# A decode kernel's TensorE loop split into two nested halves, with zero products ahead of its first tile

## The chip, the cores and the metric

The kernel runs on one core of one Trainium2 chip. The metric is device time in microseconds (us) of one execution. The spans in the profiles are about 2 us shorter than these times; they run from the first to the last instruction.

## The reference, cut to what matters

Four sequences decode one token each. Attention has 16 query heads that share 8 key/value heads, with 8192 cached positions of width 256. A small MLP branch gates the result.

```python
q = (xn @ wq)                                  # 4 x 16 heads x 256
scores = einsum("bhqd,bhkd->bhqk", q, k) * 256 ** -0.5
o = einsum("bhqk,bhkd->bhqd", softmax(scores), v)
s = o @ wo
g = silu(mlp(xn))                              # w3, w4 (448 x 1792, 1792 x 448)
return x + s * g
```

There are 4 x 8 = 32 pairs of sequence and key/value head; "head h" below means one of these, 0 to 31. Each needs 4 MB of K and 4 MB of V, and these make up nearly all of the 279 MB that the kernel reads.

## The kernel before: the parts that matter

One queue (SyncE) issues all large loads in program order. There are two buffers for K and two for V. A K load for head h may be issued only when head h-2 has been transposed and evacuated, that is, copied out of TensorE's output memory by VectorE or ScalarE (`v_k` counts this).

```python
def load_k(h):
    if h >= 2:
        sp.wait_ge(S["v_k"], h - 1)
    sp.dma_start(kn_dst(h), A_k_cache[b, g]...)         # 4 MB
...
load_k(0); load_k(1)
load_wo(NLATE, HQ, "dwo")                               # 2.6 MB
for h in range(2, NH):
    load_k(h)
    load_v(h - 2)
# ... cut: the last two V loads, and the last 0.9 MB of wo
```

TensorE transposes K in 16 groups of 8 tiles (`f_t`, which takes the K semaphore at group 0), multiplies the transposed tiles with q (`f_s`), and runs the V products of head h-2 (`f_pv`) at the end of the body. Its loop holds two heads, and the last section, `finish()`, lies inside the loop. The 17th turn runs it and every other turn jumps over it.

```python
def body(h):
    for j in range(NGR):                                # 16 groups
        f_t(h, j)
        if j >= LAG: f_s(h, j - LAG)
        # ... cut: small f32 products of head h-1
    # ... cut: the last f_s, interleaved with f_pv(h - 2, ...)

with nc.Fori(0, NH // 2 + 1, engines=[e], head_slot={e: 64}) as it:
    with pe.If(it != NH // 2):
        body(0)
        body(1)
    with pe.If(it == NH // 2):
        finish()
```

`head_slot` is a parameter for where the loop's first instruction is placed.

## Time and profile before

| quantity | before | where read |
|---|---|---|
| time, median of the first 3 runs | 661.8 us | timed runs |
| span of the profiled run | 658.8 us | page |
| bytes read | 279 MB, 424 GB/s | page |
| TensorE busy | 84% | page, part 1 |
| distance from head to head, heads 6 to 31 (median) | 19.43 us | timeline |
| distance between landings of 4 MB loads in that stretch | 9.71 us (432 GB/s) | landing records |

**Which engine limits.** The DMA queue does. TensorE's busy share is high, but before nearly every head TensorE waits for that head's K. This is the list of waits of the kernel before (engine, line, what it waited for: total us, times, longest):

```profile
PE pst L582 <- PEq L243: 84.9, 29, 6.5
```

The reader is to see 29 waits, nearly one per head. Line 243 is the helper that records every semaphore wait, so the line does not say which wait it was. The trace's landing records do (each 4 MB load has 16 landing records there, and its landing is the last of the 16): from head 6 on each of these waits ends 0.14 us after the landing of that head's K. With a wait of 1.8 to 4.6 us per head, TensorE work saved in the middle of the run only lengthens the wait.

**Where the queue ran dry.** The timeline of TensorE in the kernel before shows two odd places (columns: start us, us, engine, line, operation, output<-inputs, shape, count, [idle before <- releaser]):

```profile
23.67 0.60 PE L572 MATMUL psm<-ou_f,selb 128*32 128x112 f32 x8 [0.82 <-PEq L243]
30.80 1.87 PE L582 MATMUL pst<-ident_b,kn 128*128 128x128 bf16 x16 [6.53 <-PEq L243]
...
48.18 1.05 PE L582 MATMUL pst<-ident_b,kn 128*128 128x128 bf16 x16
...
66.01 0.27 PE L602 MATMUL psm<-ident_f,rmax 128*2 128x128 f32 x1
72.75 1.87 PE L582 MATMUL pst<-ident_b,kn 128*128 128x128 bf16 x16 [6.47 <-PEq L243]
```

Head 0 starts slowly, 1.87 us for 16 transposes against 1.05 us for head 1, after 6.53 us of idle time. The clock granted to TensorE is either 0.5 or 1.0 of the full one in the trace's clock records. Here the first record is 1.0 from 37.15 us on; there is none before it. Head 2, the first after the loop's back edge, waits 6.47 us although its K had landed at 58.6 us; then it too takes 1.87 us for 16 transposes, and here the records show 0.5, from 71.28 to 78.11 us. Both delay the issue of a K load. These are the issues in SyncE's timeline, kernel before:

```profile
44.99 0.33 SPq L201 DMA_DIRECT2D kn<-in_A_k_cache_dram  x1
...
86.53 0.33 SPq L201 DMA_DIRECT2D kn<-in_A_k_cache_dram  x1
```

They are K of head 2 and K of head 4. By the landing records the loads ahead of them in the queue were complete at 47.22 us (wo) and 87.78 us (V of head 1), so each was issued only 2.23 and 1.25 us ahead. What that did can be seen in stretches of the kernel before (columns: stretch in us and its length, busy us of PE, PEld, DVE, ACT and POOL with their instructions, granted clock, DMA share, GB/s):

```profile
38.00:48.00 10.00, 10.00 (x210) 8.31 (x207) 4.57 (x9) 4.37 (x5) 0.00 (x0) 1.00 0.99 349
85.00:90.00 5.00, 5.00 (x104) 3.23 (x100) 1.97 (x4) 1.02 (x1) 0.00 (x0) 1.00 0.69 242
140.00:155.00 15.00, 12.51 (x268) 10.56 (x263) 6.98 (x15) 6.62 (x10) 0.32 (x2) 1.00 1.02 439
```

The last column is the point: 242 GB/s around 87 us against 439 later. Counted by landings, wo to K of head 2 took 11.35 us and V of head 1 to K of head 4 took 10.90 us, where 9.71 is normal. That is 1.64 + 1.19 = 2.8 us.

### The profile page before, as it was taken

The numbers are of one execution on the slowest core, as the hardware profiler recorded it, in microseconds if no ns is written. First come the engines' busy times: TensorE is split into PE (matmuls) and PEld (weight loads), VectorE is DVE, ScalarE is ACT, GpSimd is POOL, SyncE is SP. The second block draws the span as 40 slices with busy tenths as digits, with TensorE's granted clock in tenths as the row PEclk, the third lists the DMA queues.
The fourth block names the chain that finished last, engine by engine and source line by source line (L and its number), as shares of the span: only waits on it lengthen the run. The fifth ranks groups of instructions, "written<-read, shape, count | busy, mean of one in ns | idle before, by whom it ended". The sixth has DMA issues, their size and how long they took to land. (4 is left out here: it accounts for less than half of the span.)

```text
span 658.8 us, 22917 instructions
## 1 busy us (share of the span) xinstructions
PE 550.9 (84%) x9941; PEld 474.2 (72%) x9941; DVE 274.3 (42%) x593; ACT 256.1 (39%) x364; POOL 13.6 (2%) x77
## 2 busy tenths in 40 slices
PE   2499699987888988888988888998888898878896
PEld 1388588875767876676887766887676688757774
DVE  7344255543444343334443444444344344433441
ACT  4044255542334443334443433444333444423440
POOL 2000000000000000000000000000000000000000
PEclk9998799997898788799877899888789987978998
DMA  8999989999999999999999999999999999999997
GB/s 363 441 382 424 432 366 444 418 444 430 430 444 416 446 414 446 424 436 440 420 442 418 444 418 442 436 426 440 420 444 416 444 428 434 434 426 442 418 429 296
DMA packets 12369, 279.13 MB, mean 424 GB/s; under 512 B 1220, under 2 KB 3272, under 8 KB 3784
## 3 DMA queue, kind: packets, MB, share of 16 engines
q1 hardware_dynamic: 12336, 278.99, 99.0%
q8 instruction: 7, 0.11, 0.1%
q14 instruction: 2, 0.02, 0.0%
q10 hardware_dynamic: 24, 0.01, 0.0%
HBM read 278.99 MB, written 0.00 MB: 424 GB/s over the span
## 5 line engine op out<-in xcount | busy, mean ns | idle before, releaser
L582 PE MATMUL pst<-ident_b,kn 128*128 128x128 bf16 x4096 | 349.3, 240 | 84.9 <-PEq L243 84.9
L293 ACT ACTIVATE kT<-pst 128x1024 bf16<-128x1024 bf16 x224 | 229.3, 1024 | 364.5 <-ACTq L243 363.6
L582 PEld LDWEIGHTS pst<-ident_b,kn 128*128 128x128 bf16 x4096 | 277.3, 108 | 90.4 <-issue 89.8
L291 DVE COPY kT<-pst 128x1024 bf16<-128x1024 bf16 x288 | 197.5, 692 | 268.2 <-DVEq L243 268.2
L594 PE MATMUL psc<-qc,kT 128*128 128x2 bf16 x4096 | 179.0, 164 | 0.9 <-issue 0.8
L594 PEld LDWEIGHTS psc<-qc,kT 128*128 128x128 bf16 x4096 | 158.2, 98 | 29.7 <-issue 29.2
L638 PE MATMUL psv<-vb,pT 128*4 128x512 bf16 x1056 | 86.0, 378 | 1.3 <-PEq L243 1.2
L612 PE MATMUL psm<-sel,po 128*128 128x2 f32 x272 | 36.6, 257 | 0.0
L612 PEld LDWEIGHTS psm<-sel,po 128*128 128x128 f32 x272 | 34.7, 196 | 0.0
L638 PEld LDWEIGHTS psv<-vb,pT 128*4 128x4 bf16 x1056 | 21.8, 82 | 16.7 <-issue 2.0
L451 DVE TENSOR_REDUCE rmax<-psc 128x2 f32<-128x128 f32 x32 | 9.3, 292 | 48.1 <-DVEq L243 48.1
L469 DVE COPY po<-psv 128x512 f32<-128x512 f32 x34 | 23.5, 692 | 4.9 <-DVEq L243 4.1
L456 DVE TENSOR_REDUCE gmax<-psm 2x1 f32<-2x128 f32 x32 | 8.9, 279 | 35.2 <-DVEq L243 35.2
L315 ACT ACTIVATE pT<-psc,negb 128x64 bf16<-128x64 f32 x66 | 20.6, 331 | 5.4 <-ACTq L243 5.4
L606 PEld LDWEIGHTS psm<-diag,ones_f 2*128 2x128 f32 x66 | 14.0, 262 | 6.5 <-issue 5.6
L278 POOL COPY qc<-qT 128x4 bf16<-128x4 bf16 x32 | 5.9, 186 | 589.1 <-DVEq L468 573.0
L606 PE MATMUL psm<-diag,ones_f 2*128 2x2 f32 x66 | 16.7, 320 | 1.1 <-PEq L243 0.9
L315 ACT ACTIVATION_READ_ACCUMULATOR pT<-psc,negb 128x1 f32 x66 | 13.6, 206 | 0.0
L602 PEld LDWEIGHTS psm<-ident_f,rmax 128*2 128x2 f32 x32 | 2.6, 80 | 14.0 <-issue 14.0
L624 PE MATMUL psm<-rowsum,ones_f 128*128 128x2 f32 x66 | 12.0, 251 | 0.0
L533 PE MATMUL pst<-ident_b,xn_b 4*128 4x4 bf16 x14 | 0.6, 161 | 11.6 <-DVE xn_b L364 6.9
L624 PEld LDWEIGHTS psm<-rowsum,ones_f 128*128 128x128 f32 x66 | 9.8, 188 | 0.4 <-issue 0.4
(95 smaller groups left out, 96.5 us busy)
## 6 DMA issues: line engine op xcount, KB each, us to landing
kn<-in_A_k_cache_dram SPq DMA_DIRECT2D x32, 4096.0 KB, 25.6
vb<-in_A_v_cache_dram SPq DMA_DIRECT2D x31, 4096.0 KB, 30.8
vb<-in_A_wq_dram SPq DMA_DIRECT2D x1, 3584.0 KB, 11.3
vb<-in_B_w_dram SPq DMA_DIRECT2D x2, 1568.0 KB, 16.4
wo_sb<-in_A_wo_dram SPq DMA_DIRECT2D x1, 2688.0 KB, 43.8
kn<-in_A_v_cache_dram SPq DMA_DIRECT2D x1, 2048.0 KB, 25.0
kn<-in_A_v_cache_dram SPq DMA_DIRECT2D x1, 1024.0 KB, 27.0
kn<-in_A_v_cache_dram SPq DMA_DIRECT2D x2, 512.0 KB, 28.2
```

The costliest lines, as they stand in the source:

```text
L291: engine.tensor_copy(dst, src).then_inc(S["v_ev"], 1)
L293: engine.activation(dst, src, ACT.Copy).then_inc(S["a_ev"], 1)
L315: ins = act.activation(pv_p[:, :, hh], sc[:, :, hh], ACT.Exp, bias=negb[:, s, hh:hh + 1], scale=SCALE, accum_out=rowsum[:, s, hh:hh + 1])
L451: v.tensor_reduce(rmax[:, :], psc[h % 2][:, 0:NCH * REP].rearrange("p (k h) -> p h k", h=REP), AX.X, ALU.max).then_inc(S["v_rmax"], 1)
L456: v.tensor_reduce(gmax[:, :], psm[0:REP, 0:P], AX.X, ALU.max).then_inc(S["v_s"], 1)
L469: v.tensor_copy(po[:, slot], psv[:, 0:CP * DH]).then_inc(S["v_po"], 1)
L582: ins = pe.transpose(dst[:, t * P:(t + 1) * P], kn[:, h % 2, GC * j + kl, half * P:(half + 1) * P], ident_b[:, :])
L594: ins = pe.matmul(psc[h % 2][:, kk * REP:(kk + 1) * REP], kT[:, j % RING, t * P:(t + 1) * P], qc[:, h % 2, half, :], start=(half == 0), st ...
L606: pe.matmul(psm[:, P:P + REP], ones_f[0:REP, :], diag[:, :], start=True, stop=True).then_inc(S["p_m2"], 1)
L612: ins = pe.matmul(dst(dh)[:, 0:width], po[:, slot, i * DH + dh:(i + 1) * DH:NHALF], sel[:, i, 0:width], start=(i == 0), stop=(i == CP - 1))
L624: pe.matmul(psm[:, P + REP:P + 2 * REP], ones_f[:, :], rowsum[:, h % 2, :], start=True, stop=True)
L638: ins = pe.matmul(psv[o:o + CP * REP, 0:CP * DH], pT[:, h % 2, kk * REP:(kk + CP) * REP], src[:, kk:kk + CP, :].rearrange("p c d -> p (c d)"),
```

## The change

The inner loop now holds only the two bodies, so its back edge goes straight from the end of the body to its head. The jump over `finish()` comes once, after 16 heads. Eighteen matrix products with zero weights, whose result is overwritten later, fill the time in which TensorE waited for the first K. `head_slot` moves from 64 to 104 with them.

```diff
+    NWARM = 18
...
+            for i in range(NWARM):
+                pe.matmul(psv[0:PVW, 0:QW], pT[:, 0, 0:PVW], wq_sb[:, 0, 0:QW], start=True, stop=True)
...
-            with nc.Fori(0, NH // 2 + 1, engines=[e], head_slot={e: 64}) as it:
-                with pe.If(it != NH // 2):
+            with nc.Fori(0, 2, engines=[e]) as part:
+                with nc.Fori(0, NH // 4, engines=[e], head_slot={e: 104}):
                     body(0)
                     body(1)
-                with pe.If(it == NH // 2):
+                with pe.If(part == 1):
                     finish()
```

## The prediction

> **What bounds the kernel.** The DMA queue. The page gives 279 MB and 424 GB/s over a 658.8 us span. The timeline shows heads 6 to 31 starting every 19.42 us, and before each of them TensorE idles 1.8 to 4.6 us until that head's K has landed. The landings in the trace come every 9.71 us per 4 MB load, 432 GB/s. A TensorE head that does not wait takes 14.9 us (89.7 to 104.6). So nothing saved inside a steady head can show; only moments when the queue has run dry can be recovered.
>
> **Where the queue ran dry.** From the landing of the big wo load (47.2 us) to that of head 6's K (137.5 us) nine 4 MB loads landed in 90.3 us, where 9 x 9.71 = 87.4 would do: 2.9 us lost, in two places.
> 1. K of head 2 landed 11.35 us after wo, 1.65 too many. It was issued at 44.99 us, only 2.2 us before wo had landed, because head 0 ran slowly: 16 transposes take 1.87 us there against 1.05 later. The clock records show full speed only from 37.1 us. TensorE had been idle from 24.3 to 30.8 us.[...]
> 2. K of head 4 landed 10.9 us after V of head 1, 1.2 too many. It was issued at 86.5 us, just as the queue emptied, because TensorE stood from 66.3 to 72.75 us (6.47 us, timeline) at the first end of the loop body, although that head's K had landed at 58.6. The instruction queue moved a 16 KB block at 69.6 us: the jump over finish() went to a block not yet fetched, and head 2 then started at half clock. No block is fetched after 76.2 us, so later jumps are cheap (0.23 us at 105.0).
>
> **The change.** The inner loop's back edge goes from the body's end to an already loaded head, so the 6.5 us stall disappears in iteration 0; head 2 starts near 65 us at full clock and issues K of head 4 about 11.7 us later (as head 3 does), near 77 us, about 9 us before the queue is empty. The jump over finish() comes at head 16; even if it costs 6.5 us again, TensorE idles about 3 us there anyway and K is issued some 17 us before the queue needs it: no cost. The 18 zero products fill 24.3 to 30.7 us (0.43 us each at half clock, estimated from the 512-column products, so 4 to 7.7 us). At worst they delay the first tile 1.3 us; head 0 then runs at full clock and issues K of head 2 near 42.7 us, 4 to 5 us ahead of the queue's end.
>
> **Time.** On the critical path: 1.65 + 1.2 = 2.85 us. Everything later moves forward by that; the end (last V pieces and wo, DMA paced) is unchanged. 661.8 - 2.8 = 659.0 us; 8 in 10: 657.4 to 661.0. Chances: faster by over 2% 0.01, within 2% 0.98, slower 0.01.
>
> **What would show it.** First 16 transposes about 1.1 us; no gap near 66 us; head 2 about 8 us earlier; K of head 2 landing near 57, of head 4 near 96; still 19.42 us per head; waits for K per head unchanged or longer. Perhaps one long wait near head 16.
>
> **What would make it wrong.** The zero products not lifting the clock; instruction blocks arriving every 7.1 us holding the now faster first pass[...]; the shifted loop no longer staying resident, with fetches each iteration.

Two passages are cut, where marked, because no trace or run shows them: a rule about the clock, and a figure for how long the work of one instruction block takes. (The lengths of half-clock stretches that went with the rule are measured; they stand below, at the first gap.) No term of the sum went with them: it is 1.65 + 1.2 = 2.85 us, as printed.

## The result

The median was 658.55 us (658.05 to 660.08, 4 runs) against 661.62 us (660.52 to 662.67, 4 runs). The ratio is 0.9958, 95% interval [0.9933, 0.9982]. Here and below a ratio is the mean time of one kernel's runs over that of the other's of the same rounds, so it is not quite the ratio of the medians. This is a real gain of about 0.4%.

TensorE's timeline after the change, same columns as before:

```profile
25.20 5.34 PE L578 MATMUL psv<-vb,pT 128*32 128x512 bf16 x18
30.86 1.05 PE L586 MATMUL pst<-ident_b,kn 128*128 128x128 bf16 x16 [0.32 <-PEq L244]
...
45.95 1.05 PE L586 MATMUL pst<-ident_b,kn 128*128 128x128 bf16 x16
...
65.61 0.27 PE L606 MATMUL psm<-ident_f,rmax 128*2 128x128 f32 x1
65.72 1.06 PE L586 MATMUL pst<-ident_b,kn 128*128 128x128 bf16 x16
```

The zero products took 5.34 us and delayed the first tile by 0.06 us. Head 0 runs at full speed (1.05 us for 16 transposes; the records show 1.0 from 27.81 to 55.11 us). Head 2 follows head 1 without a gap. The two K loads are issued earlier (SyncE's timeline, kernel after):

```profile
42.76 0.33 SPq L202 DMA_DIRECT2D kn<-in_A_k_cache_dram  x1
...
77.44 0.33 SPq L202 DMA_DIRECT2D kn<-in_A_k_cache_dram  x1
```

They are now 4.70 us ahead of wo's landing (47.46 us) and 8.90 us ahead of the landing of V of head 1 (86.34 us). The queue stays full (stretches of the kernel after):

```profile
38.00:48.00 10.00, 9.70 (x196) 7.70 (x194) 4.82 (x11) 3.95 (x4) 0.19 (x1) 1.00 1.09 415
85.00:90.00 5.00, 5.00 (x109) 5.00 (x107) 2.19 (x5) 3.12 (x4) 0.00 (x0) 1.00 1.00 433
```

The landings wo to K of head 2 and V of head 1 to K of head 4 now both took 9.72 us. Head 4's K landed at 96.06 us instead of 98.69, and the last piece of wo, the last load of all, at 652.37 us instead of 655.22, which is 2.85 us earlier. (In the second profile of the kernel before, shown further down, it was 653.55 us.)

**A loss at the end.** The span of this profiled run fell only from 658.8 to 658.0 us. The time from the last landing to the end grew from 3.5 to 5.7 us. In `finish()` TensorE waits for the V of head 30; here is that place in the timelines, first before, then after:

```profile
643.08 1.90 PE L638 MATMUL psv<-vb,pT 128*4 128x512 bf16 x32 [1.15 <-PEq L243]
644.91 0.38 PE L624 MATMUL psm<-rowsum,ones_f 128*128 128x2 f32 x2
645.15 2.02 PE L612 MATMUL psm<-sel,po 128*128 128x2 f32 x16
```

```profile
640.29 3.58 PE L642 MATMUL psv<-vb,pT 128*4 128x512 bf16 x32 [2.59 <-PEq L244]
643.81 0.59 PE L628 MATMUL psm<-rowsum,ones_f 128*128 128x2 f32 x2
644.26 3.55 PE L616 MATMUL psm<-sel,po 128*128 128x2 f32 x16
```

After a longer idle stretch (2.59 us against 1.15) the same work takes nearly twice as long (3.58 us against 1.90): the clock records show half clock from 638.8 to 652.4 us. This run was the slowest of the four (span 658.0; the others 656.0, 656.1 and 657.0). That the longer wait brought the half clock on is not shown. In two later profiles of the same kernel (labels rep_after, rep_after2) the tail took 3.62 and 4.28 us, and in the second profile of the kernel before (rep_before), with half clock from 648.65 us on, 4.19 us. So the tail differed by up to 2.1 us between profiles of the changed kernel and by 0.7 us between the two of the kernel before. The longest, 5.68 us, came with 13.65 us of half clock in the last section, where the first profile of the kernel before has 3.41 us (from 648.13 us on) and a tail of 3.53. How much of the scatter of the timed runs this explains was not shown.

### The profile page after: what moved, and what is told of

It is laid out like the page before. It is cut to its first block, busy times and chain, and to the rows that moved or that the text cites. A ratio compares the mean times of both kernels' runs of the same rounds, so it can differ in the third digit from the quotient of the medians.

```text
span 658.0 us, 22911 instructions
## 1 busy us (share of the span) xinstructions
PE 555.3 (84%) x9959; PEld 475.0 (72%) x9959; DVE 276.3 (42%) x593; ACT 256.1 (39%) x364; POOL 13.4 (2%) x77
## 5 line engine op out<-in xcount | busy, mean ns | idle before, releaser
L616 PE MATMUL psm<-sel,po 128*128 128x2 f32 x272 | 38.2, 263 | 0.0
L616 PEld LDWEIGHTS psm<-sel,po 128*128 128x128 f32 x272 | 36.2, 204 | 0.0
```

Of the source, the lines that this page charges most:

```text
L616: ins = pe.matmul(dst(dh)[:, 0:width], po[:, slot, i * DH + dh:(i + 1) * DH:NHALF], sel[:, i, 0:width], start=(i == 0), stop=(i == CP - 1))
```

## The experiments

The theory: the time lost was the queue's, and what counts is only how long before the queue runs empty a K load is issued. Four rivals: (A) one half of the change brings all the gain; (B) each jump over the last section costs something, so the 15 saved jumps pay all along; (C) the shift of the loop within the instruction blocks pays; (D) TensorE's own lost time counts, so a higher clock or a removed stall pays as such.

### The changed kernel again

No edit.

> The changed kernel again, beside its parts on the same chip. Theory: 2.9 us under before (ratio 0.9956). K of head 2 lands near 57.2 us, K of head 4 near 96.1 us, last late wo piece near 652.4 us. Spread of about 2 us between runs comes from the clock of TensorE after the last load: in a good run the span ends 3.6 us after the last landing, in a bad one 5.6 us.

658.65 us (6 runs) against 660.57 (11 runs): ratio 0.9971 [0.9953, 0.9990]. In the profile K of head 2 landed at 56.94, K of head 4 at 95.79 and the last piece at 652.35 us, and the tail took 3.62 us, all as expected. That the clock is what sets the tail was the theory; this run shows the tail alone. The ratio is smaller than expected, because the kernel before scattered from 658.40 to 662.39 us.

### Zero products alone, with the one loop

```diff
+    NWARM = 18     # and the 18 products, as in the change
-            with nc.Fori(0, NH // 2 + 1, engines=[e], head_slot={e: 64}) as it:
+            with nc.Fori(0, NH // 2 + 1, engines=[e], head_slot={e: 104}) as it:
```

> Zero products and head slot 104, the one loop and its jump over the last section as before. Theory: K of head 2 lands near 57.2 us (1.4 us earlier than before's 58.6); TensorE still stands at the first end of the body, until a block fetched at about 67 us has come, so head 2 starts near 70 us, K of head 4 is issued at 82 to 84 us, 2.5 to 4.5 us before the queue is empty, and lands at 96.1 to 97.2. Total 1.7 to 2.8 us under before. Rival A (the loop alone brings the gain, as the stall is the larger wait): within 0.5 us of before. Rival C (moving the loop's slot brings it): all of 2.9.

K of head 2 landed 9.71 us after wo, at 57.06: the first gap is gone. Head 2 started at 69.27 us, after 3.13 us of idle time in place of 6.47. K of head 4 was issued at 82.31 us as expected, 3.9 us ahead, and landed 9.71 us after V of head 1. So in this profile the products removed both gaps: with them the stall before head 2 also ended earlier, at 69.27 us in place of 72.75. The time gained less: 659.45 us, ratio 0.9982 [0.9962, 1.0002], 1.2 us by the means, below the 1.7 to 2.8 expected. Whether other executions issued the later K too late, or lost time at the end, is not known.

### The nested loop alone

```diff
-                with nc.Fori(0, NH // 4, engines=[e], head_slot={e: 104}):
+                with nc.Fori(0, NH // 4, engines=[e], head_slot={e: 64}):
-    NWARM = 18
+    NWARM = 0
```

> Nested loop at head slot 64, no zero products. Theory: first 16 transposes 1.87 us as before, K of head 2 lands at 58.6 as before; no stall at 66 us; head 2 starts near 66.5 and K of head 4 is issued near 78 and lands near 97.4 (before 98.7); total 1.2 to 1.5 us under before. Rival A (loop alone brings all): 2.9 us under. Rival B (each of the 15 saved jumps saves time in every iteration): heads after 6 closer than 19.42 us apart.

Head 2 started at 64.87 us with no gap and K of head 4 landed 9.72 us after V of head 1: the second gap is gone, as expected. The first was expected to stay at 1.6 us and was only 0.38 us: the first 16 transposes took 1.86 us, but the next 16 took 1.58 us and not 1.89, so the clock came up about 3 us sooner than in the profile before, without any product to bring it. 659.06 us, ratio 0.9983 [0.9962, 1.0004], again 1.2 us by the means. Heads stayed 19.4 us apart, against rival B. Each half alone gives 1.2 us and both together gave 1.9 us in the same rounds. The intervals are too wide to order the three kernels, but rival A gets no support from them. In the two profiled runs either half alone brought most of the gain: the last piece landed at 652.19 us (products alone) and 652.90 us (loop alone), where it was 655.22 before and 652.35 with both.

### The shift of the loop alone

```diff
-            with nc.Fori(0, NH // 2 + 1, engines=[e], head_slot={e: 64}) as it:
+            with nc.Fori(0, NH // 2 + 1, engines=[e], head_slot={e: 104}) as it:
```

> The kernel before with head slot 104 in place of 64 and nothing else. Theory: same as before within 0.5 us (K of head 2 near 58.6, the stall near 66 us stays, K of head 4 near 98.7). Rival C (it is where the loop lies in the fetch blocks): faster by up to 2.9 us.

660.25 us, ratio 0.9990 [0.9970, 1.0009]. The stall was 5.61 us, K of head 2 landed 11.12 us after wo and K of head 4 11.27 us after V of head 1. Both gaps stayed, so rival C falls.

### All jumps kept, but over blocks that are fetched before they matter

```diff
             with nc.Fori(0, NH // 2 + 1, engines=[e], head_slot={e: 64}) as it:
+                with pe.If(it == NH // 2):
+                    finish()
                 with pe.If(it != NH // 2):
                     body(0)
                     body(1)
-                with pe.If(it == NH // 2):
-                    finish()
```

> The one loop of 17 turns with its jump in every turn, but the last section lies ahead of the body in the program, so the jump over it comes first at the loop's entry, while TensorE waits for K of head 0 anyway; no zero products, slot 64. Theory (the stall near 66 us is the wait for a block that was not yet fetched, not the jump itself): no gap over 1 us at the start of head 2 although all 16 jumps are still there; K of head 4 issued near 76 to 79 us and no late landing (V of head 1 to K of head 4 9.7 us, before 10.9); time as for the nested loop alone, 1.2 to 1.5 us under before. Rival B (a jump costs each time): a gap of some us stays at head 2, time as before.

Half of it came as expected. All 16 jumps are still there, and the stall at head 2 is gone (timeline):

```profile
68.77 0.27 PE L602 MATMUL psm<-ident_f,rmax 128*2 128x128 f32 x1
68.88 1.06 PE L582 MATMUL pst<-ident_b,kn 128*128 128x128 bf16 x16
```

K of head 4 landed 9.72 us after V of head 1. So it was not the jump that cost 6.5 us, but the jump to a block that had not come yet. The fetches agree: in the five profiles that stall at head 2 (before, rep_before, slot_only, k_halves, warm_only) TensorE goes on 3.2 to 3.3 us after the packet of an instruction block has started, at 69.59 us in the kernel before. The time was a miss, however: 664.81 us, ratio 1.0067 [1.0049, 1.0086], slower. The wait for a block had moved into head 0:

```profile
33.02 0.50 PE L582 MATMUL pst<-ident_b,kn 128*128 128x128 bf16 x3
35.78 1.57 PE L582 MATMUL pst<-ident_b,kn 128*128 128x128 bf16 x13 [2.26 <-issue]
```

With that and the slow start (1.86 us for the first 16 transposes), K of head 2 was issued at 48.09 us, 0.8 us after wo had landed, and landed 14.06 us after it: 4.35 us late. The miss speaks for the theory: TensorE stood less here than in the kernel before (2.26 and, in head 1, 1.13 us, in place of 6.47), and the kernel is slower, because the loss fell where the queue had the least in hand. That explains the profiled run, whose last piece landed at 656.59 us, 1.4 us later than before. It was the fastest of the six (662.24 us; the others took 663.88 to 666.04 us), and what the others lost beyond it is not known.

### Seven jumps in place of one

```diff
-            with nc.Fori(0, 2, engines=[e]) as part:
-                with nc.Fori(0, NH // 4, engines=[e], head_slot={e: 104}):
+            with nc.Fori(0, 8, engines=[e]) as part:
+                with nc.Fori(0, NH // 16, engines=[e], head_slot={e: 104}):
-                with pe.If(part == 1):
+                with pe.If(part == 7):
```

> The changed kernel with 8 outer by 2 inner turns: seven jumps over the last section in place of one, the first after head 3, when its block has been fetched. Theory: same as the changed kernel within 0.5 us, heads 6 to 31 still 19.42 us apart, landings wo to K of head 6 87.4 us. Rival B (a jump costs each time): slower than the changed kernel by up to half of what before loses.

658.79 us, ratio 0.9981 [0.9961, 1.0001]. The landings from wo to K of head 6 took 87.61 us (87.46 in the changed kernel, 90.30 before), and the last piece landed at 652.35 us, as in the changed kernel (652.37 and 652.35). Rival B falls: six more jumps moved the landings by 0.15 us at most.

### Twice as many zero products

```diff
-    NWARM = 18
+    NWARM = 36
```

> The changed kernel with 36 zero products in place of 18: the clock is up as well, but the first tile comes 3.5 to 4 us late. Theory (only how long before the queue's end a K load is issued counts: about 3.8 us are needed after the wo load, from the runs so far): K of head 2 issued near 46.7 us, 0.5 us before wo has landed, and landing near 60.2, 3.3 us late; K of head 4 not late; total 3 us over the changed kernel, about as slow as before or slower, though TensorE is at full clock from the first tile. Rival D (what pays is the higher clock as such, by TensorE finishing its work sooner): as fast as the changed kernel, for TensorE waits for K in every later head anyway.

665.12 us, ratio 1.0055 [1.0032, 1.0078]: slower than before. The timeline:

```profile
25.20 10.44 PE L578 MATMUL psv<-vb,pT 128*32 128x512 bf16 x36
35.58 1.07 PE L586 MATMUL pst<-ident_b,kn 128*128 128x128 bf16 x16
```

The first tile runs at full speed (1.07 us for 16 transposes), 4.8 us late. K of head 2 was issued at 48.03 us, 0.70 us after wo had landed, and landed 4.22 us late. Compare the run above with `finish()` first: a slow start and a stall of 2.26 us there, 16 transposes in 1.07 us here, the same issue time (48.09 and 48.03 us), and the same loss (4.35 and 4.22 us). Rival D falls: the clock counts only through the issue time.

There was a second loss that was not expected. From K of head 6 to the last landing this run took 520.41 us, where all the others above took 517.4 to 517.9. The DMA view counts the instruction blocks; first the kernel before, then this run:

```profile
q8 instruction: 7, 0.11, 0.1%
```

```profile
q8 instruction: 17, 0.28, 0.2%
```

Nine of the ten additional blocks came between 334.9 and 385.4 us, around and after the half-time jump; the tenth came at 657.1 us. Head 16 began only at 345.0 us, after 13.26 us of idle time, and one later K (head 18), issued 2.6 us ahead of the queue's end, landed 1.2 us late. Why these blocks were moved is not shown.

### K loads issued in halves, TensorE's program untouched

This goes back to the kernel before, and changes only when K is issued.

```diff
 def load_k(h):
-    sp.wait_ge(S["v_k"], h - 1)                  # for h >= 2
-    sp.dma_start(kn_dst(h), ...)
+    for i in range(2):
+        sp.wait_ge(S["v_k"], 2 * (h - 2) + i + 1)
+        sp.dma_start(kn_dst(h)[:, lo:hi], ...)   # 2 MB each
 # VectorE: v_k is raised after group 8 too; TensorE takes 32 of dk in place of 16
```

> The kernel before, TensorE's program unchanged (slot 64, one loop, no zero products), but each K load is issued in two halves of 2 MB, the first when the first 9 of 16 groups of the head two before have been evacuated. Theory (only how long before the queue's end a K load is issued counts): the stall of 5 to 6.5 us near 66 us and the slow first tiles (1.87 us for 16) stay, but the first half of K of head 2 is issued near 39 us and that of head 4 near 80 us, both over 5 us before the queue is empty; wo to K of head 2 and V of head 1 to K of head 4 take 9.7 us each, wo to K of head 6 87.4 us; 2 to 3 us under before, as fast as the changed kernel. Rival D (TensorE's own lost time counts): as before.

At the start the theory held to the letter. The stall stayed (6.04 us before head 2), the first 16 transposes took 1.86 us, and yet the two gaps were gone: the halves were issued from 39.0 and 81.1 us on, and K of head 2 landed 9.78 us after wo, K of head 4 9.79 us after V of head 1. V of head 1 landed at 86.65 us, 1.1 us earlier than before. These are the two pairs of issues (each line spans both halves):

```profile
39.02 6.30 SPq L203 DMA_DIRECT2D kn<-in_A_k_cache_dram  x2
...
81.06 6.02 SPq L203 DMA_DIRECT2D kn<-in_A_k_cache_dram  x2
```

So an earlier issue, with TensorE's stall and slow start left as they were, removes the gaps. The total was a miss: 660.19 us, ratio 1.0000 [0.9984, 1.0016]. The timeline shows where it went; first the kernel before, then this one, two successive late heads each:

```profile
137.65 1.05 PE L582 MATMUL pst<-ident_b,kn 128*128 128x128 bf16 x16 [2.87 <-PEq L243]
...
157.08 1.87 PE L582 MATMUL pst<-ident_b,kn 128*128 128x128 bf16 x16 [4.57 <-PEq L243]
```

```profile
135.58 1.05 PE L587 MATMUL pst<-ident_b,kn 128*128 128x128 bf16 x16 [0.57 <-PEq L246]
155.08 1.86 PE L587 MATMUL pst<-ident_b,kn 128*128 128x128 bf16 x16 [4.64 <-PEq L246]
```

A head now takes 19.50 us in place of 19.43. This kernel is 2.1 us ahead at head 6 (135.58 against 137.65), and pays that lead back head by head: from the landing of K of head 6 to that of head 30 it took 468.1 us, against 466.6 us before. In the end its last piece landed at 654.65 us, against 655.22 before, and the 0.6 us that are left vanish in the scatter.

### The version that was meant to beat both

The first edit adds ten more zero products, this time in `finish()`, while TensorE waits for the V of head 30:

```diff
                 take(pe, "v_po")
+                for i in range(10):
+                    pe.matmul(psv[0:PVW, 0:D], pT[:, 0, NCH * REP:NCH * REP + PVW],
+                              wo_sb[:, HQ - 1, 0, :], start=True, stop=True)
                 take(pe, "dv%d" % ((h - 1) % 2), 16)
```

> The changed kernel with 10 more zero products (448 columns) in the last section while TensorE waits for the V of head 30. Theory (the spread of the changed kernel's time, spans 656.0 to 658.0, is TensorE at half clock in the last section after an idle stretch): the time from the last landing to the end is 3.6 us in nearly all runs, spans 655.9 to 656.6, median 0.3 to 0.6 us under the changed kernel and a smaller spread. Rival: spread unchanged[...].

658.03 us (657.77 to 659.27), ratio 0.9965 [0.9949, 0.9981]. The profiled run had a tail of 3.53 us. Spans were 655.7 to 657.2 us; four of the six lie at or below 656.0. The three ratios of the changed kernel are 0.9958, 0.9971 and 0.9976, so an advantage over it is not shown: it would be some tenths of a microsecond. Nor is the smaller spread that was expected: 1.5 us here, and 1.2, 2.0 and 2.0 us in the three sets of the changed kernel.

The second adds the K loads in halves to that.

> The changed kernel with the K loads in halves and the 10 zero products of the last section: no late K in any run and the clock held at the end. Theory: spans 655.8 to 656.5 in nearly all runs, median 0.3 to 0.6 us under the changed kernel of the same rounds; the halves alone add nothing to the changed kernel, whose queue never runs dry at the start.

660.53 us, ratio 1.0000 [0.9984, 1.0016]: slower than the changed kernel beside it, and a miss. The halves could add nothing at the start, as said, and their 0.08 us per head was left out of the expectation. The clock was not held at the end either: in this profile, with the ten products in place, it fell to half at 649.83 us and the tail took 3.91 us. The changed kernel in the same rounds:

> The changed kernel once more, to stand beside the two kernels with K in halves on the same chip: spans 656.0 to 658.0, ratio to before 0.995 to 0.998; landings wo to K of head 6 in 87.4 us.

658.80 us, ratio 0.9976 [0.9958, 0.9993]; wo to K of head 6 took 87.64 us, 0.2 us more than expected, because K of head 3 landed 0.22 us late although it was issued 4.97 us ahead.

### The kernel before, a second profile

No edit; one execution, state unknown.

> The kernel before once more, for a second profile of it. Theory: K of head 2 and K of head 4 land late by an amount that follows from how long before the queue's end they were issued (about 3.8 us minus that time after wo, 2.4 us minus it after V of head 1, from the runs so far); [...]the two amounts may differ from 1.6 and 1.2 us.

The stall was 6.42 us again, but the second 16 transposes took 1.70 us (1.89 in the first profile), so the clock came up earlier, and K of head 2 was issued 3.63 us ahead and landed only 0.23 us late. K of head 4 was 1.07 us late. Together that is 1.3 us, against 2.8 in the first profile. The K loads of heads 2 and 4, sorted by how far ahead of the queue's end they were issued (landing of the load ahead minus the issue; "late" is the distance of the two landings minus 9.71). Left out are the K loads in halves and those whole loads that were issued 4.4 us or more ahead, except of the changed kernel's first profile; these landed at most 0.03 us late:

| load | kernel (label) | issued ahead, us | late, us |
|---|---|---|---|
| K of head 2, after wo | finish_first | -0.79 | 4.35 |
| | warm36 | -0.70 | 4.22 |
| | before | 2.23 | 1.64 |
| | slot_only | 2.29 | 1.41 |
| | loop_only | 3.39 | 0.38 |
| | rep_before | 3.63 | 0.23 |
| | rep_after | 4.05 | 0.02 |
| | after | 4.70 | 0.01 |
| K of head 4, after V of head 1 | slot_only | 0.84 | 1.56 |
| | before | 1.25 | 1.19 |
| | rep_before | 1.70 | 1.07 |
| | warm_only | 3.93 | 0.00 |
| | after | 8.90 | 0.01 |

For each of the two loads the lateness follows the issue time, whatever delayed TensorE. About 4 us ahead was enough (3.93 us: 0.00 late; 4.05 us: 0.02 late). Nearer than that, ahead and late add up to 3.5 to 3.9 us for K of head 2, so nearly every microsecond is lost, and to 2.4 to 2.8 us for K of head 4. Why the two loads differ is not known. Small delays come without a late issue too: in four profiles (before, rep_before, rep_after2, warm36) K of head 3 landed 0.17 to 0.24 us late, though it had been issued 5 to 7 us ahead. The straight lines in the expectation fit roughly: for rep_before they give 0.2 and 0.7 us, where 0.23 and 1.07 were measured.

## Why the prediction was right, point by point

- **The bound.** Right. Heads stayed 19.43 us apart (median). The list of waits after the change still has 29 waits on this line:

```profile
PE pst L586 <- PEq L244: 76.5, 29, 4.6
```

  The two waits named above shrank by 12.7 us together (6.53 to 0.32 and 6.47 to nothing), but the sum fell only by 8.4: the other waits grew by 4.3 us, and the time fell by about 3. The loads came at 432 GB/s (one of 4 MB every 9.71 us) in both kernels, and from head 6 on every head started 0.14 us after its K had landed, so a saturated queue is the plain reading.
- **The first gap.** Right. The zero products took 5.34 us (forecast 4 to 7.7), the first 16 transposes 1.05 us (1.1), K of head 2 was issued at 42.76 us (42.7) and landed at 57.17 us (57). The 18 zero products agree with the forecast's sizes: by the trace they start 0.43 us apart at first and 0.22 us from 27.8 us on, where the clock records go from 0.5 to 1.0, 2.6 us after the first of them. (The kernel before shows both rates: its 512-column products start, four at a time, every 0.42 us from 12.6 us on, L543, and every 0.21 us from 643 us on, L638.) But for the last one, which the end of the record cuts off, the half-clock stretches last 3.41 us or whole multiples of it in the traces before and after. The clock also fell without an idle stretch of that length: TensorE stood for only 0.83 of the 3.41 us before the drop at 57.63 us in the kernel before, and not at all before the drop at 649.83 us in k_halves_both. What decides is not known.
- **The second gap.** Right. No gap near 66 us; head 2 at 65.72 us (65); K of head 4 issued at 77.44 (77), landing at 96.06 us (96). The experiment with `finish()` ahead of the body shows that the stall was the wait for an instruction block and not the jump's own cost.
- **The jump at half time.** Right that it would be free; the one long wait that "perhaps" would come there did not: 3.16 us before head 16, as in the kernel before. An instruction block was fetched at 329.7 us, after the jump.
- **The risk of the first pass.** It came about without harm. TensorE, at full clock until 55.11 us, stood 2.43 us in head 1, until 56.0 us. That it waited for an instruction block is read from the timing: in all profiles the stalls of over 0.45 us inside the first three heads end 2.2 to 2.6 us after the packet of an instruction block has started (here at 53.70 us). K of head 3 was still issued 4.4 us ahead of the landing of V of head 0 and was not late.
- **The sum.** 2.85 us was forecast for the critical path, and the last landing of the profiled run moved by 2.85 us. That it agrees so closely is in part luck of the pair: against the second profile of the kernel before it moved by 1.2 us. As a mean over runs it was too large: the three ratios give 2.8, 1.9 and 1.6 us. What was mis-sized is the term of 1.65 us for the first gap. It was read from one profile, and the second profile of the same kernel has 0.23 us there, because the clock came up earlier. The four profiles in which head 0 starts without zero products and is not held up further (before, slot_only, loop_only, rep_before; whole K loads) have 0.9 us there as a mean; with a mean of 1.3 us for the second gap (before, slot_only, rep_before) an estimate of the sum is 2.2 us, and the mean of the three measured gains is 2.1. What the kernel before loses varies (658.40 to 662.67 us over 37 runs in four sets of rounds), while in the three profiles of the changed kernel K of heads 2 and 4 were never more than 0.02 us late, and it stays within 657.78 to 660.08 us (16 runs).
- **"The end is unchanged."** This step failed for the profiled run: the tail after the last landing grew by 2.1 us, as TensorE dropped to half clock in `finish()` (from 638.8 us on). The tail varies in both kernels (3.53 and 4.19 us before; 5.68, 3.62 and 4.28 us after), so whether the change makes it longer as a mean is not shown.

## What to carry to other kernels

In a kernel bound by one DMA queue, look for the moments when the queue is empty and ask who issued the next load late. Here microseconds of TensorE were worth something only there, and the worth was settled by how far ahead of the queue's end the load was issued (K of head 2: 2.23 us ahead, 1.64 us late; 4.05 us ahead, 0.02 us late). The first run through a code path stalled on its instructions here (6.47 us at head 2 of the kernel before), so let that happen where the engine waits anyway, and then look where the next block's wait has gone: with `finish()` ahead of the body it moved into head 0 (2.26 us), and the kernel became slower (ratio 1.0067). Before sizing a gain from one profile, take a second one: in two profiles of the kernel before the first gap was 1.64 and 0.23 us, and the second 16 transposes took 1.89 and 1.70 us.

## What else the traces measured

- In the kernel before, seven instruction blocks of 16 KB were moved on queue q8, the last at 76.18 us. None followed up to the end, across 15 further back edges of a loop whose turn has over 570 products (256 transposes, 256 with q, 64 with V).
- In the first pass, beside a full DMA queue, these blocks started 6.4 to 12.1 us apart in the kernels before and after (7.1 us in three of the six cases before). TensorE stood up to 2.43 us at a time inside a head, which the timing puts down to a block, and the jump to a block still on its way cost up to 6.47 us.
- With one core running, loads landed at 432 GB/s for over 500 us (one of 4 MB every 9.71 us).
- An issue about 4 us ahead of the landing of the load before it kept the queue full to within 0.25 us, and one 0.8 to 2.3 us ahead cost 1.1 to 1.6 us.
- In the full queue, 2 MB loads in place of 4 MB for K made a head 0.08 us longer (19.50 against 19.43 us).
